# Gated linear attention and a GELU MLP on one core: two more pairs' q' and k' transposed by DMA, their decays computed a block earlier

## The chip, the cores and the metric

The kernel runs on one NeuronCore of a Trainium2 chip. The metric is the device time of one execution in microseconds (us), lower is better. Beside it stands a profile: one execution recorded by the hardware profiler, with every instruction of every engine. The engines are TensorE (PE; its weight loads are listed as PEld), VectorE (DVE), ScalarE (ACT), GpSimd (POOL) and SyncE (SP). SP and POOL only issue DMAs here, apart from a few small instructions of POOL. Each engine runs its own list of instructions strictly in the order in which they were emitted.

## The reference, cut to what matters

Inputs are q, k, v and alpha, each of shape 4 x 8 x 768 x 48 (batch, heads, steps, head size), and two weight matrices, 384 x 2048 and 2048 x 384.

```python
for t in range(S):
    state = alpha[:, :, t, :, None] * state + einsum('bhd,bhe->bhde', k[:, :, t], v[:, :, t])
    y[:, :, t] = einsum('bhd,bhde->bhe', q[:, :, t], state)
x = y.transpose(0, 2, 1, 3).reshape(B * S, H * D)
h = x @ w_in
g = 0.5 * h * (1.0 + tanh(c * (h + 0.044715 * h**3)))
return g @ w_out
```

A recurrence with a decay per step and channel runs over 768 steps; its outputs, 8 heads x 48 = 384 numbers a step, go through a two-layer MLP with GELU.

## The kernel before, in words

The 768 steps are cut into six chunks of 128. A *pair* is one chunk of two batches, so there are 12 pairs, numbered m = 0 to 11. For each pair the recurrence is turned into matrix products:

- `ln` and `exp` (ACT): la = ln(alpha), summed over the steps by a triangular product (`cum`, PE), then b = exp(cum), binv = exp(-cum), and bend, the decay over the whole chunk. `ln` and `exp` need another activation table than GELU, and a table load stands between.
- `qp`, `kp` (DVE): q' = q b and k' = k binv (line 408).
- `turn`: q' and k' are transposed, head channels to partitions. For most pairs TensorE does it, 16 transposes of 128 x 128 for a pair (line 418), and DVE or ACT copies the result out of PSUM (`ev`, line 436). For the pairs in `TURN_QK` (7 to 11 before) SP issues two DMA transposes instead (`turn_dma`, line 456), one for q' and one for k'; TensorE and DVE then do nothing for it.
- `attn` (PE, line 479): scores of k' and q' within the chunk; `mask` (DVE, line 486) makes them triangular; `y` (PE, lines 533 and 536) adds the part of the state and the part within the chunk; `kv` (PE, line 496) and `st` (DVE, lines 518 and 521) carry the state on.
- `x`: y is copied to bf16 (line 543) and transposed, either by TensorE with a DVE copy (`tx`, `xe`, lines 550 and 554) or, for the pairs in `TURN_X`, by a DMA transpose from SP (line 462).
- The MLP for the pair's 256 tokens, called a *block*: `l1` (line 562), eight groups of six products, each followed by a GELU of 128 x 512 on ACT (line 568); `l2` (line 581), 32 products of 128 x 384, then a copy `ot` (line 593) and a store from SP (line 599).

The order of instructions isn't written as loops. `tasks()` makes a list of tasks with a cost for each engine that may run it, a priority, the tasks it depends on, and the buffers that it takes. `Scheduler.order()` then plays the engines against each other with these costs and emits the tasks in the order in which they would start. The priority of attention work of pair m is about 100 m, that of the MLP is 10000 and more, so that attention work goes first as soon as it can and the MLP fills the rest. The first part of the program (to about 31 us) is not planned but written out, in `FIRST`: `P:fill.5` there means five products of zeros on TensorE. After that the planner puts in products of zeros itself where it sees TensorE idle, up to its time 60 us.

Three tables set what the change is about. `DECAYS` says after which block's GELUs the `ln` and `exp` of which pairs are run: `4: (6, 7)` means that pairs 6 and 7 follow the last GELU of block 4, and the first GELU of block 5 waits for them. `TURN_QK` and `TURN_X` choose the crossbar of the DMA or TensorE for the transposes. The planner's guess when a DMA transpose has landed is in `put`:

```python
if t.kind in ("turn", "store"):
    xbar = t.done = max(xbar, t.end + W["landed"] - t.xbar) + t.xbar
    t.done += t.late
```

with 1250 ns for the issue, 2200 for `landed`, and `late` on top. On the chip the instruction that reads the result waits for the DMA's semaphore, whatever the planner guessed.

The inputs come in by DMAs that POOL issues (line 298: a, q, k and v of a pair), one after the other, until about 91 us. Buffers bound how far they run ahead: six of `a`, five each of `q` and `k`, six of `vb`; q' and k' live in rings of four (`qp`, `kp`), the transposed q' and k' in four of `qkT`, the sums of ln(alpha) in one PSUM buffer `ca`.

Of the kernel before, what the change touches and what calls it, by code (L numbers as in the profile page):

```python
# [14 lines left out]
W = dict(**{'in': 2400},  # L15
    ln=760, exp=720, bend=170, gelu4=510, gelu2=340, table=1290,
    cum=530, cum_packed=1500, t8=450, t4=225, attn=340, kv=170, inter=170, intra=205, tx=168, l1_4=655, l1_2=340, l2=655,
    qk2=910, qk1=500, ev8=650, ev4=350, mask=640, st=1090, st0=545, end=110, attn2=590, vb=320, vb_act=480, ring=1300, ring_issue=670, out=2050, lead=600, receipt=1400, receipt_hw=1000, xc=520, xe=330, ot=540,
    ev8_act=960, ev4_act=520, xc_act=450, xe_act=450, ot_act=450,
    strip=1700, cast=1900, weight=2080, dma=2100, issue=1100, wissue=760, sp=100, store=2600, turn=1250, landed=2200, xbar_qk=1500, xbar_x=1000, late_x=2500, late_qk=1200, piece=330, late_k=1500, piece_issue=450, begin=620, cast_0=1300, share=1200, cast_1=1900, ln_packed=1040, cold=380, fill=216, zero=1100,  # L20
)
COST = {
    ("ACT", "b"): (385, 135), ("ACT", "binv"): (385, 135), ("ACT", "ev"): (600, 40), ("ACT", "gelu"): (510, 110),
# [148 lines left out]
class _Kernel:  # L172

    BLOCKS = ((0,), (1,), (2,), (3,), (4,), (5,), (6,), (7,), (8,), (9,), (10,), (11,))
    DECAYS = {-1: (0, 1), 1: (2, 3), 2: (4,), 3: (5,), 4: (6, 7), 5: (8,), 6: (9,), 7: (10,), 8: (11,)}

    SPLIT = (2,)
    EARLY = (0, 1)
# [3 lines left out]
    RINGS = (('a', 0, 0, 1), ('a', 0, 1, 2), ('q', 0, 0, 1), ('k', 0, 0, 1), ('q', 0, 1, 2), ('k', 0, 1, 2),  # L182
             ('a', 1, 0, 1), ('a', 1, 1, 2), ('q', 1, 0, 1), ('k', 1, 0, 1), ('q', 1, 1, 2), ('k', 1, 1, 2))
    FIRST = """
        A:table.0 S:load.0 S:load.1 S:load.2 S:load.3 S:load.4 A:ln0.0 S:load.5 P:fill.5 P:cum0.0 A:ln0.1 G:gate.0 G:load.12 S:load.6 P:cum0.1 A:b0.0 S:load.7
        A:binv0.0 V:qp0.0 A:bend0.0 A:b0.1 V:kp0.0 S:load.8 P:fill.2 P:t0.0 A:bend0.1 A:binv0.1 V:ev0.0 P:t0.1 S:load.9 A:ev0.1 S:load.10 V:qp0.1 P:fill.3
        P:attn0.0 V:kp0.1 P:t0.2 G:gate.1 S:load.11 G:load.13 V:mask0.1 P:fill.1 P:t0.3 G:load.14 A:ev0.3 V:end0.0 V:ev0.2 A:ln1.0 V:mask0.0 P:fill.4
        P:attn0.1 G:load.15 P:cum1.0 V:mask0.2 A:vb0.0 G:load.16 A:ln1.1 V:vb0.1 P:y0.0 V:mask0.3 A:b1.0 P:cum1.1 G:load.17 A:x0.0 V:qp1.0 A:binv1.0 P:y0.1
# [13 lines left out]

    NARROW = (0, 1)

    TURN_QK, TURN_X = (7, 8, 9, 10, 11), (6, 7, 8, 9, 10, 11)

    EV_ACT = (0, 1, 2, 3)

# [393 lines left out]
    def tasks(self):  # L602
        s = self.s = Scheduler(self.BUFS, self.fill, 60000, self.FIRST, self.LANDED)
# [6 lines left out]
        loads, n, gate, held = {}, 0, [], {}  # L610
# [26 lines left out]
        for step in self.LOADS:  # L637
            if step[0] == "v":
                rows(int(step[1:]), "v")
            elif step[:4] == "gate":  # L640
                r, m, j = step[4:].split()
                m, j = int(m), int(j)
                gate = [s.add("gate", {"POOL": 150}, n, self.wait(r, m, j), [loads[r, m, j]] if (r, m, j) in loads else [])]
# [10 lines left out]
        for m, (c, i) in enumerate(pairs):  # L654
            u, P = self.p[c, i], 100 * m
# [5 lines left out]
            for lo, hi in self.parts(m):  # L661
                n = hi - lo
                ln = s.add("ln", {"ACT": W["ln_packed" if u["packed"] else "ln"] * n // 2}, P, self.ln(u, lo, hi), [loads["a", m, lo]], LN_EXP)
                cum = s.add("cum", {"PE": W["cum_packed" if u["packed"] else "cum"] * n // 2}, P - 400, self.cum(u, lo, hi), [ln])
                x = [s.add(e, {"ACT": W[e] if e == "bend" else W["exp"] * n // 2}, P + 2 + j, self.exp(u, e, lo, hi), [cum], LN_EXP)
                     for j, e in enumerate(("b", "binv", "bend") if u["sums"] else ("b", "binv"))]
                cums.append(cum)
                exps += x
                lns[m].append(ln)
                if u["sums"]:  # L670
                    be.append(x[2])
                ends[m].append(x[-1])
                step = 1 if early else n
                for j in range(lo, hi, step):
                    qp[j:j + step] = [s.add("qp", {"DVE": W[f"qk{step}"]}, P + (5 + 4 * j if u["packed"] else 5 + 5 * j), self.scaled(u, "q", j, j + step),
                                            [x[0], loads["q", m, j]])] * step
                for j in range(lo, hi, step):
                    kp[j:j + step] = [s.add("kp", {"DVE": W[f"qk{step}"]}, P + (6 + 4 * j if u["packed"] else 6 + j), self.scaled(u, "k", j, j + step),
                                            [x[1], loads["k", m, j]])] * step
            for r, ts in (("qp", qp), ("kp", kp)):  # L680
                for j in range(2):
# [14 lines left out]
            exps[0].take("b8", *qp, *kp)  # L696
            vs, kvs, tq, cs, users, turns, masks = [], [], [], [], [], [], {}
            if m in self.TURN_QK:
                tq = [s.add("turn", {"SP": W["turn"]}, P + 10, self.turn_dma(u, n), d, xbar=W["xbar_qk"], late=W["late_qk"] * (m < 8)) for n, d in (("q", qp), ("k", kp))]
                owner, turned = tq[0], tq  # L700
            backs = []
            vin = [loads["v", m, j] for j in range(2)]
# [4 lines left out]
            for j in range(2):  # L707
                o, k = P + 10 + 3 * j, kp[j]
                if m not in self.TURN_QK:
                    turned = []  # L710
                    o -= 3 * u["packed"]
                    for which in ("q", "k") if early else ("qk",):
                        n = 4 * len(which)
# [22 lines left out]
            for j in range(2):  # L736
                b, o, k, ms, turned = 2 * i + j, P + 10 + 3 * j, kp[j], masks[j], turns[j]
# [16 lines left out]
                if c < NCH - 1:  # L754
                    if u["packed"]:
                        tb = s.add("t", {"PE": W["t4"]}, P + 29 + j, self.turn_back(u, j), turned)
                        k = s.add("ev", {"DVE": W["ev4"], "ACT": W["ev4_act"]}, P + 29 + j, self.turned_back(u, j), [tb])
# [30 lines left out]
        n = 0  # L788
        f, gs, l2s, ots, parts_of, firsts = {}, {}, {}, [], [], []
        between = {m: [x for p in self.DECAYS.get(m, ()) for x in ends[p]] for m in range(-1, len(self.BLOCKS))}  # L790

# [17 lines left out]
        def layer2(m):  # L809
            nonlocal n  # L810
            s.scope = m
            units = [(pairs[p][0], 2 * pairs[p][1] + j) for p in ((0, 1) if m == 0 else self.BLOCKS[m]) for j in range(2)]
            parts = range(self.NFT // 4)
            first = {}
            for u, part in ([(u, part) for part in parts for u in units] if m == 0 else [(u, part) for u in units for part in parts]):
                c, b = u
                t = s.add("l2", {"PE": W["l2"]}, 10000 + n, self.layer2(f, c, b, part),
                          gs[m if m else b // 2][2 * part:2 * part + 2] + [loads["w", "out", part]] + firsts, stream=n - 16)
                l2s.setdefault(c, []).append(t)
                n += 1  # L820
                first.setdefault(u, t)
                if (c, b) == (NCH - 1, B - 1):
                    t.deps += gs[m]
                    if part % 2 == 0:
                        parts_of.append(t)
                    if part % 2:
                        ot = s.add("ot", {"DVE": W["ot"], "ACT": W["ot_act"]}, -1, self.result(f, c, b, part // 2), [t])
                        ots.append((ot, s.add("store", {"SP": W["sp"]}, n, self.store(f, c, b, part // 2), [ot])))
                        parts_of[part // 2].take("ff", ot)
                        if part == 3:  # L830
                            ots[0][0].take("ot", *[x[1] for x in ots])
                elif part == parts[-1]:
                    ot = s.add("ot", {"DVE": W["ot"], "ACT": W["ot_act"]}, -1, self.result(f, c, b), [t])
                    first[u].take("ff", ot)
                    ot.take("ot", s.add("store", {"SP": W["sp"]}, n, self.store(f, c, b), [ot]))

        for m in range(len(self.BLOCKS)):
            layer1(m)
            if m:
                layer2(m if m > 1 else 0)  # L840
        for m, ps in self.DECAYS.items():
            for p in ps if m >= 0 else ():
# [57 lines left out]
```

## Time and profile before

| What | Value |
|---|---|
| median of three runs | 179.37 us (179.23, 179.37, 179.83) |
| the profiled execution's own time | 179.62 us |
| its span, first to last instruction | 177.8 us |
| granted TensorE clock, mean | 0.997 |
| layer 1, 576 products of 128 x 256 | 68.8 us busy |
| layer 2, 400 products | 69.4 us busy |
| GELU, 96 of 128 x 512 | 56.1 us busy |
| transposes of q' and k' by TensorE, 112 | 227 and 226 ns each, 5.7 us busy for each of q' and k' |
| activation table loads, 18 | 1283 ns each |
| a load of a, q, k or vb issued by POOL | 11.7 to 12.2 us to landing (median) |

How to read it: busy time is summed for an engine, and the engines work side by side, so the shares don't add up to the span. A product listed at 273 ns overlaps the one behind it; what it costs TensorE is the distance from its start to the next one's start, which the chain of work that ended last shows better. Time to landing is counted from when the DMA's issue starts.

### The profile page before, as it was taken

To read this page: it belongs to the slowest core of one execution; us is meant where nothing else is said; L and a number is where in the kernel's file an instruction comes from. 1 tells how busy PE (TensorE), PEld (TensorE's weight loads), DVE (VectorE), ACT (ScalarE), POOL (GpSimd) and SP (SyncE) were. 2 spreads that over 40 slices of the span, in tenths; PEclk is the share of its full clock that TensorE was granted. 3 is DMA by queue.
4 is the path that set the end of the run, shared out by engine and by line. 5 is a ranking of instruction groups with operands and counts; after the bars stand their busy time and mean duration, and the time that the engine had idled before them with its cause. 6 is when DMAs were issued, how large, how long until landed. Compare 5 with 4: busy or idle time off the path is not lost.

```text
span 177.8 us, 4409 instructions
## 1 busy us (share of the span) xinstructions
PE 172.0 (97%) x1829; PEld 136.1 (77%) x1831; DVE 95.0 (53%) x187; ACT 130.8 (74%) x216; POOL 58.0 (33%) x64
## 2 busy tenths in 40 slices
PE   5999999999999999999999999999999999999992
PEld 1756899666896897798698689688697697786972
DVE  6399820254967894597499797495426405000000
ACT  4558899875898668858788967987988984481831
POOL 2377536996647676667640000000000000000000
PEclk9999999999999999999999999999999999999998
DMA  4999999999999999999999993271270360401102
GB/s 124 277 253 198 196 233 232 224 240 197 231 295 195 219 269 217 191 254 210 195 248 237 197 168 85 55 177 48 46 208 4 89 162 4 129 4 48 44 3 86
DMA packets 48901, 28.86 MB, mean 162 GB/s; under 512 B 37489, under 2 KB 45297, under 8 KB 48881
## 3 DMA queue, kind: packets, MB, share of 16 engines
q0 software_dynamic: 26464, 17.70, 60.7%
q1 hardware_dynamic: 22416, 10.88, 24.7%
q8 instruction: 14, 0.23, 0.6%
q14 instruction: 7, 0.05, 0.1%
HBM read 25.17 MB, written 4.72 MB: 168 GB/s over the span
## 4 chain that ended last, share of the span: by engine, by line
PE 90%; DVE 3%; ACT 3%; issue 1%; POOL 0%; POOLq 0%
PE acc L581 35%; PE hT L562 34%; PE at L479 4%; PE qkT_ps L418 4%; PE yps L536 2%; PE cum L368 2%; PE yps L533 2%; PE kv L496 2%; PE cum L336 2%; PE idle L279 1%; DVE atm L486 1%; ACT qkT L436 1%; PE xT_ps L550 1%; ACT L568 1%; PE cum L370 1%
## 5 line engine op out<-in xcount | busy, mean ns | idle before, releaser
L581 PE MATMUL acc<-w_out,gT 128*128 128x384 bf16 (+1 forms) x400 | 69.4, 320 | 0.0
L562 PE MATMUL hT<-xT,w_in 128*128 128x256 bf16 x576 | 68.8, 273 | 0.1
L568 ACT ACTIVATE gT<-hT 128x512 bf16<-128x512 f32 x96 | 56.1, 599 | 15.1 <-PE hT L562 11.6
L562 PEld LDWEIGHTS <-w_in 128*128 128x128 bf16 x576 | 61.2, 113 | 1.5 <-issue 0.2
L581 PEld LDWEIGHTS <-gT 128*128 128x128 bf16 x400 | 36.5, 97 | 18.9
L486 DVE TENSOR_TENSOR atm<-at,ut 128x512 bf16<-128x512 f32 x48 | 30.2, 684 | 13.9 <-PE at L479 13.9
L408 DVE TENSOR_TENSOR qp<-q,b 128x768 bf16<-128x768 f32 (+1 forms) x15 | 11.9, 795 | 17.9 <-ACT b L397 17.9
L593 ACT COPY ot<-acc 128x384 f32<-128x384 f32 (+1 forms) x18 | 8.3, 460 | 13.8 <-PE acc L581 11.5
L298 POOL DMA_DIRECT2D q<-in_q_dram x11 | 12.2, 1108 | 7.3 <-DMA w_out<-in_moe_w_out_dram 1.9
L298 POOL DMA_DIRECT2D k<-in_k_dram x11 | 12.3, 1119 | 6.6 <-DMA vb<-in_v_dram 2.2
L298 POOL DMA_DIRECT2D vb<-in_v_dram x11 | 12.1, 1103 | 5.8 <-DMA a<-in_alpha_dram 2.0
L298 POOL DMA_DIRECT2D a<-in_alpha_dram x11 | 12.2, 1113 | 5.4 <-DMA w_in<-in_moe_w_in_dram 1.3
L397 ACT ACTIVATE b<-cum 128x768 bf16<-128x768 f32 (+1 forms) x15 | 10.2, 683 | 3.1 <-PE cum L340 1.6
L270 ACT ACT_TABLE_LOAD x9 | 11.5, 1283 | 0.9 <-PEq L884 0.7
L408 DVE TENSOR_TENSOR kp<-k,binv 128x768 bf16<-128x768 f32 (+1 forms) x15 | 11.9, 791 | 0.0
L568 ACT ACT_TABLE_LOAD x9 | 11.5, 1283 | 0.2
L397 ACT ACTIVATE binv<-cum 128x768 bf16<-128x768 f32 (+1 forms) x15 | 10.2, 681 | 0.0
L518 DVE TENSOR_TENSOR stmp<-kv,st 128x384 f32<-128x384 f32 x16 | 8.9, 553 | 2.0 <-PE kv L496 2.0
L543 DVE CAST x<-yps 128x384 bf16<-128x384 f32 x12 | 6.7, 558 | 5.2 <-PE yps L536 5.2
L351 ACT ACTIVATE la<-a 128x768 f16<-128x768 f32 (+1 forms) x11 | 8.5, 783 | 1.1 <-DMA a<-in_alpha_dram 1.0
L521 DVE TENSOR_TENSOR st<-stmp,ends 128x384 bf16<-128x384 f32 x16 | 8.9, 558 | 0.6
L436 ACT COPY qkT<-qkT_ps 128x512 bf16<-128x512 bf16 (+1 forms) x9 | 6.5, 728 | 3.6 <-PE qkT_ps L418 3.5
(64 smaller groups left out, 158.8 us busy)
## 6 DMA issues: line engine op xcount, KB each, us to landing
out_dram<-ot SPq DMA_DIRECT2D x23, 192.0 KB, 2.4
a<-in_alpha_dram POOLq DMA_DIRECT2D x9, 384.0 KB, 12.2
q<-in_q_dram POOLq DMA_DIRECT2D x9, 384.0 KB, 11.7
k<-in_k_dram POOLq DMA_DIRECT2D x9, 384.0 KB, 11.8
vb<-in_v_dram POOLq DMA_DIRECT2D x9, 192.0 KB, 11.9
w_in<-in_moe_w_in_dram POOLq DMA_DIRECT2D x4, 384.0 KB, 9.2
w_out<-in_moe_w_out_dram POOLq DMA_DIRECT2D x4, 384.0 KB, 11.7
a<-in_alpha_dram SPq DMA_DIRECT2D x4, 192.0 KB, 4.0
```

The costliest lines, as they stand in the source:

```text
L270: nc.scalar.add_instruction(mybir.InstLoadActFuncSet(name=nc.get_next_instruction_name(), act_func_set_id=i, engine=mybir.EngineType.Activ ...
L298: dma(u[t][:, lo:hi].rearrange("t b h d -> t (b h) d"), src.rearrange("b h s d -> s (b h) d")[c * C:(c + 1) * C])
L351: self.nc.scalar.activation(u["la"][:, lo:hi, :, 0:self.D], u["a"][:, lo:hi], AF.Ln)
L397: self.nc.scalar.activation(u[n].rearrange("t i h d -> t i (h d)")[:, lo:hi], cum, AF.Exp, scale=1.0 if n == "b" else -1.0)
L408: self.nc.vector.tensor_tensor(out, rows, b, op=ALU.mult)
L486: self.nc.vector.tensor_tensor(u["atm", i][:, o], u["at", i][o], self.ut[:, None, :].to_broadcast([self.C, self.H // 2, self.C]), op=ALU.mult)
L518: nc.vector.tensor_tensor(s, acc, old, op=ALU.add)
L521: nc.vector.tensor_tensor(new.rearrange("f p (o d) -> f (p o) d", o=2), acc.rearrange("f p (o d) -> f (p o) d", o=2), ends, op=ALU.mult)
L562: self.nc.tensor.matmul(h[:, s], w_in[:, j, nt % 4 + s], self.xT[c % self.NX][:, j, lo:hi].rearrange("p g t -> p (g t)"), start=j == 0, st ...
L568: return lambda e: self.nc.scalar.activation(self.gT[c % self.NG][:, nt:nt + 2, lo * self.C:hi * self.C], f.pop(("h", c, lo, nt)), AF.Gelu ...
L581: self.nc.tensor.matmul(f["acc", c, b][:, lo:hi], self.gT[c % self.NG][:, nt, b * self.C:(b + 1) * self.C], self.w_out[:, nt, lo:hi], star ...
L593: self.copy(e)(f["ot", c, b][:, sl], f["acc", c, b] if half is None else f["acc", c, b, half][:, sl])
```

## The change

The `ln` and `exp` of pair 5 are moved from after block 3 to after block 2, beside those of pair 4; those of pair 6 from after block 4 to after block 3; those of pair 7 stay after block 4, now alone. The q' and k' of pairs 5 and 6 are transposed by DMA. The x of pair 6, which was transposed by DMA, is transposed by TensorE. The `qp` and `kp` tasks of pairs 5 and 6 get a priority that is 90 lower in number, which is near that of the pair before. The planner's `late` is 7500 ns for q' and k' of pairs 5 and 6 and 3500 for those of pair 7, in place of 1200 for pair 7 alone. The first group of products of zeros has seven in place of five.

```diff
-    DECAYS = {-1: (0, 1), 1: (2, 3), 2: (4,), 3: (5,), 4: (6, 7), 5: (8,), 6: (9,), 7: (10,), 8: (11,)}
+    DECAYS = {-1: (0, 1), 1: (2, 3), 2: (4, 5), 3: (6,), 4: (7,), 5: (8,), 6: (9,), 7: (10,), 8: (11,)}
...
-        A:table.0 S:load.0 S:load.1 S:load.2 S:load.3 S:load.4 A:ln0.0 S:load.5 P:fill.5 P:cum0.0 A:ln0.1 G:gate.0 G:load.12 S:load.6 P:cum0.1 A:b0.0 S:load.7
+        A:table.0 S:load.0 S:load.1 S:load.2 S:load.3 S:load.4 A:ln0.0 S:load.5 P:fill.7 P:cum0.0 A:ln0.1 G:gate.0 G:load.12 S:load.6 P:cum0.1 A:b0.0 S:load.7
...
-    TURN_QK, TURN_X = (7, 8, 9, 10, 11), (6, 7, 8, 9, 10, 11)
+    TURN_QK, TURN_X = (5, 6, 7, 8, 9, 10, 11), (7, 8, 9, 10, 11)
+
+    AHEAD = {5: 90, 6: 90}
+    LATE = {5: 7500, 6: 7500, 7: 3500}
...
-                    qp[j:j + step] = [s.add("qp", {"DVE": W[f"qk{step}"]}, P + (5 + 4 * j if u["packed"] else 5 + 5 * j), self.scaled(u, "q", j, j + step),
+                    qp[j:j + step] = [s.add("qp", {"DVE": W[f"qk{step}"]}, P - self.AHEAD.get(m, 0) + (5 + 4 * j if u["packed"] else 5 + 5 * j), self.scaled(u, "q", j, j + step),
...
-                    kp[j:j + step] = [s.add("kp", {"DVE": W[f"qk{step}"]}, P + (6 + 4 * j if u["packed"] else 6 + j), self.scaled(u, "k", j, j + step),
+                    kp[j:j + step] = [s.add("kp", {"DVE": W[f"qk{step}"]}, P - self.AHEAD.get(m, 0) + (6 + 4 * j if u["packed"] else 6 + j), self.scaled(u, "k", j, j + step),
...
-                tq = [s.add("turn", {"SP": W["turn"]}, P + 10, self.turn_dma(u, n), d, xbar=W["xbar_qk"], late=W["late_qk"] * (m < 8)) for n, d in (("q", qp), ("k", kp))]
+                tq = [s.add("turn", {"SP": W["turn"]}, P + 10, self.turn_dma(u, n), d, xbar=W["xbar_qk"], late=self.LATE.get(m, 0)) for n, d in (("q", qp), ("k", kp))]
```

The entry `late_qk=1200` goes out of the table of costs.

More of the change, by code (lines that the diff above doesn't have):

```diff
@@ L19 @@
     ev8_act=960, ev4_act=520, xc_act=450, xe_act=450, ot_act=450,
-    strip=1700, cast=1900, weight=2080, dma=2100, issue=1100, wissue=760, sp=100, store=2600, turn=1250, landed=2200, xbar_qk=1500, xbar_x=1000, late_x=2500, late_qk=1200, piece=330, late_k=1500, piece_issue=450, begin=620, cast_0=1300, share=1200, cast_1=1900, ln_packed=1040, cold=380, fill=216, zero=1100,
+    strip=1700, cast=1900, weight=2080, dma=2100, issue=1100, wissue=760, sp=100, store=2600, turn=1250, landed=2200, xbar_qk=1500, xbar_x=1000, late_x=2500, piece=330, late_k=1500, piece_issue=450, begin=620, cast_0=1300, share=1200, cast_1=1900, ln_packed=1040, cold=380, fill=216, zero=1100,
 )
```

## The prediction

> **What bounds the kernel now.** I read the page first: the busy shares, the forty slices, the chain that ended last.
>
> ```profile
> span 177.8 us, 4409 instructions
> ...
> PE 172.0 (97%) x1829; PEld 136.1 (77%) x1831; DVE 95.0 (53%) x187; ACT 130.8 (74%) x216; POOL 58.0 (33%) x64
> ...
> PE   5999999999999999999999999999999999999992
> ...
> DMA  4999999999999999999999993271270360401102
> ...
> PE 90%; DVE 3%; ACT 3%; issue 1%; POOL 0%; POOLq 0%
> ```
>
> TensorE has no idle slice between the first and the last, and it is 90% of the chain; the DMA engines are as full over the first 24 slices (to 107 us). A busy TensorE may still hide stalls, so I took the busy time by stretch, and then the chain around one pair.
>
> ```profile
> 60.00:75.00 15.00, 15.00 (x172) 12.24 (x170) 10.38 (x21) 11.93 (x17) 9.65 (x9) 1.00 1.30 228
> 75.00:89.00 14.00, 14.00 (x170) 11.24 (x169) 9.62 (x20) 10.26 (x16) 9.34 (x9) 1.00 1.53 218
> ```
>
> (Columns: length, then busy of PE, weight loads, DVE, ACT, POOL; granted clock, DMA share, GB/s.) TensorE is never idle there. In the chain the sixth pair (pair 5, counted from 0) reads:
>
> ```profile
> 74.45 0.66 PE hT L562 x6
> 75.10 0.89 PE qkT_ps L418 x16
> 76.00 0.66 PE hT L562 x6
> 76.65 0.17 PE kv L496 x4
> 76.82 0.65 PE hT L562 x6
> 77.48 0.55 PE at L479 x16
> ```
>
> Sixteen transposes cost 0.89 us, 56 ns each, with layer-1 products (109 ns each) straight before and behind: product after product. So from 23 us to the last product, at 174.6 us, an instruction taken off TensorE is its issue time gained, if nothing it waits for comes later.
>
> The start is different: there the chain names products that run slowly.
>
> ```profile
> 7.17 0.88 PE idle L279 x2
> 8.04 0.85 PE qkT_ps L418 x8
> 8.90 1.04 PE idle L279 x3
> ...
> 14.79 0.38 PE idle L279
> ```
>
> Two products of zeros take 0.88 us (0.44 each) and eight transposes 0.85 (106 ns, against the 56 ns above). By the timeline four such products take 1.03 us at 10.87. The array runs at half speed until some time between 9 and 10.9 us; the windows view doesn't show that (it says 1.00 there), the durations do.
>
> **What the Trainium skill says.** (1) "TensorE: Matmul & The Clock Gate", Part 1: the array starts at half clock and is released after about 3.4 us of sustained activity, counted in windows that run freely. The trace agrees in kind: 0.44 us a product, then about 0.22. (2) "DMA: Bandwidth & Descriptors", section "Queues, rings and completion order": each DMA engine takes turns between the queues that have work for it. That bears on transposes among loads; the trace shows only SP's stores there (6.2 to 7.5 us to land against 2.1 later), which fits. No other page decides anything below.
>
> **The change part by part.**
>
> *q' and k' of pairs 5 and 6 by the crossbar.* TensorE loses 2 x 16 transposes (L418): 2 x 0.89 = 1.78 us. DVE loses four evictions (L436, 0.69 us each). SP gains four transposes, 1.2 to 1.4 us of issue each; its stores are too sparse there (57.2, 61.1, 71.9, 75.1, 85.9) for them to be pushed late by more than about that. *x of pair 6 back on TensorE* (TURN_X): 2 x 3 transposes, "0.17" each three by the chain, +0.34 us; DVE gains two copies (L554, 0.35 each), SP loses two transposes. Net: TensorE -1.78 + 0.34 = -1.44 us; DVE -2.76 + 0.70 = -2.1 us, off the chain.
>
> *Decays a block earlier* (DECAYS). The nine phases of ln and exp, each with two table loads of 1.28 us, stay nine: pair 5 joins pair 4's, pair 6 and pair 7 get one each. ScalarE can't run GELU in a phase, so TensorE lives on what doesn't need it. Now pair 4's phase is 53.51 to 61.07 (table load to table load), of which 1.41 us is idle ("issue"). The two-pair phase at 82.61 to 89.90 is 7.29 us and the single one at 68.66 to 73.46 is 4.80, so a second pair costs 2.5 us; against 1.41 idle the phase grows by about 1.1 us. TensorE's work beside it is layer 2 of block 2 (32 products of 162 ns, 5.2 us), pair 3's y and x, two cums, pair 4's transposes, and layer-1 groups as banks allow; two-pair phase 82.61 shows no TensorE idle with the same mix. Cost 0 to 0.9 us, taken 0; the phase around 83 us gives 2.5 us of ScalarE back. Buffers: `ca` has one buffer, so pair 5's cum waits for pair 4's exps (0.89 us in the phase at 83), inside the phase. Pair 5's alpha was issued at 41.85 and a load takes 12 to 13 us, so it is there at about 54.8, just in time for ln at about 55.5; q and k follow by 58.5.
>
> *AHEAD*: pair 5's qp and kp (0.95 us each on DVE) get the priority of pair 4's. They may delay an eviction or mask of pair 4 by up to 0.95 us; TensorE has layer-1 work then. Taken 0, at worst 0.5.
>
> *LATE, the new wait.* Scores (L479) of pairs 5 and 6 now wait for a DMA. In line 110 a transpose counts as done 1.25 (issue) + 2.2 us after it starts, plus `late`: 7.5 gives 10.95 us from issue. TensorE runs in order: if it lands later, layer 1 and 2 behind the scores wait too. Pair 5's k' is issued at about 63 to 64 (its b and binv at about 60, then DVE), scores due about 75; now they run at 77.4. What is known among loads:
>
> ```profile
> out_dram<-ot SPq DMA_DIRECT2D x1, 192.0 KB, 7.5
> ...
> xT<-x SPq DMA_TRANSPOSE x1, 5.9
> ...
> qkT<-qp SPq DMA_TRANSPOSE x1, 2.8
> qkT<-kp SPq DMA_TRANSPOSE x1, 2.7
> ```
>
> (The store issued at 57.2, the x transpose at 95.1 while loads still flow, and q', k' at 116 without them.) Loads add 5.4 us to a store (7.5 - 2.1) and 3.6 to an x transpose (5.9 - 2.3). From below: 2.8 + 3.6 = 6.4 us; from above, with q' before k' and one such delay each, 2.8 + 2 x 5.4 = 13.6 from the first issue, some 12 from the second. Against 10.95 I take "lands in time": stall 0, with up to 1 us in the range and the worse end as a rival. Pair 7's 3.5 gives 6.95 us, and its transposes go out near the end of the loads (the last were issued at 90 and take 10 to 12); taken 0. The four transposes also take turns from the loads; those of pairs 8 to 11 land 10 us and more before their ln, so that costs nothing.
>
> *Seven products of zeros.* Five take 1.19 to 3.50; then TensorE idles 0.76 us until the mask and la are ready at 4.26. Two more at 0.43 end their streaming at about 4.18: cost 0 to 0.1. In return TensorE is busy without a break from 1.19 instead of from 4.26. If the release then comes before 7.0 instead of at 9 to 10, the two products at 7.17 cost 0.44 instead of 0.88: the transposes, started at 7.84, are then bound by kp (done at 7.37) and start at 7.43; the first four take 0.22 instead of 0.43. DVE's first eviction moves from 8.51 to about 7.9: 0.6 us, handed on by the chain of DVE, ScalarE and TensorE up to 23 us, and with qp of the first pair the gate that lets the weights be loaded moves too. Where the free-running window falls decides it: 0 to 0.9, taken 0.6.
>
> *Sum* against the profiled execution: 177.8 - 1.44 - 0.6 = 175.75 us of span. Around the span lie 179.62 - 177.8 = 1.82 us: 177.57. The median of the runs (179.37) is 0.25 under the profiled one: 177.3; forecast **177.4 us**.
>
> **The rivals.**
>
> *Late landing (slower).* The place: TensorE at the scores of pairs 5 and 6. For it: at 103.4 us, after the loads, a 16 KB instruction fetch of 1.4 us fell on one DMA engine. Counted in 0.1 us steps, the packet records show the q' transpose moving 504 packets of 256 bytes, about 32 on each of 16 engines, then almost nothing until 105.5. So a transpose waits for its slowest engine every 32 packets or so. q' and k' of a pair are 64 + 64 per engine: four rounds. Loads add 4.1 to 5.4 us to a store on its slowest engine; if every round paid that, k' would land 19 us or more after q' was issued, some 17 after its own issue, against 10.95: 6 us late. Against it: the 24 packets per engine of the x transpose at 95 went through with 3.6 us of delay in all, and rounds may overlap. At half that, about 2.5 to 3 us per pair: 177.4 + 5 = **182.5 us**. It decides once both stalls together exceed 2 us.
>
> *Given back.* The two-pair phase costs its 0.9, a landing is 0.5 to 1 us late and the clock isn't released earlier: -1.44 + 0.9 + 0.7 = +0.2 us: **179.4**. For it: three terms that the profile can't exclude. Against: no TensorE idle in the two-pair phase that exists.
>
> *The plan isn't what the diff says.* All queues are planned anew, so a different order of loads or a fill product (0.22 us each, only before 60 us) may appear: 0.2 to 0.4 us either way, inside the ranges.
>
> **How the numbers follow.** In time and released earlier: 0.53, own range 176.6 to 178.3. Given back: 0.11, 178.3 to 180. Late landing: 0.36, 180 to 185. About 0.3% (0.54 us) is what a measurement of this kernel can tell from no change: 178.83 to 179.91. Faster takes the first case and a quarter of the second, 0.55; same 0.08; slower 0.37. For 8 in 10 the range leaves out a few hundredths below 176.6 and reaches up through most of the late case: 176.6 to 183.
>
> **What would show it.** L418 with 32 transposes fewer for q and k, L550 with 6 more. TensorE busy 100% in every stretch from 46 to 103: right; a wait of at (L479) on a DMA, or an idle gap at 74 to 78 or 86 to 92: the late rival, of the size of the gap. q' and k' transposes on SP at about 62 to 64 and 73 to 76 with times to landing under 11 us: right. The first transposes of q at about 7.4 instead of 7.84 and products of 0.22 us before 8: the start's 0.6. The forecast is wrong if k' of pair 5 takes over 12 us to land, or if GELU after the two-pair phase starts with TensorE idle.

## The result, and the profile after

The changed kernel takes 192.03 us (median of six runs, 190.19 to 199.60) against 179.56 us for the kernel before beside it: a ratio of 1.068, interval 1.062 to 1.073. The forecast was 177.4 us, and its range ended at 183.0. Some executions of a kernel, whichever it is, run some per cent longer than the rest, here those of 196.69 and 199.60 us: the ratios and intervals in this document leave such executions out, the medians don't. The profiled execution was the one of 199.60 us, so the profile shown is from a second set of runs of the same kernel (192.83 us, ratio 1.074, interval 1.070 to 1.079; its profiled execution took 193.34 us). The change has put three lines in ahead of the code, so its line numbers stand three above those before: 421 the transposes, 459 the DMA transposes of q' and k', 482 the scores, 565 and 584 layers 1 and 2.

The page after. The rows with forty characters are slices of 4.8 us here.

```profile
span 191.6 us, 4368 instructions
...
PE 174.8 (91%) x1807; PEld 135.7 (71%) x1807; DVE 92.8 (48%) x185; ACT 130.5 (68%) x216; POOL 57.9 (30%) x64
...
PE   7999999999999998299992299999999999999993
...
PEclk9999999999999999979999559999999999999999
DMA  4999999999999999999999983614327053220102
...
PE 77%; DMA 16%; ACT 3%; DVE 1%; issue 0%
```

TensorE has two holes, at slices 16 and 21 to 22. Behind each, the granted clock falls (the 7, then 5 and 5). In the chain of work that ended last TensorE's share has fallen from 90% to 77%, and a DMA holds 16%. TensorE is busy for 2.8 us longer, although it runs 22 products fewer: it has less work and does part of it at a lower clock. The windows say the same in numbers (columns as in the prediction: length, busy of PE, weight loads, DVE, ACT and POOL, then granted clock, DMA share, GB/s).

```profile
75.00:89.00 14.00, 9.27 (x100) 7.32 (x99) 6.07 (x13) 6.17 (x10) 3.44 (x3) 0.88 1.46 181
...
103.00:117.00 14.00, 8.16 (x72) 4.97 (x73) 3.14 (x6) 2.82 (x6) 0.00 (x0) 0.63 1.06 143
...
80.80:84.20 3.40, 3.37 (x27) 2.26 (x20) 3.32 (x6) 0.60 (x1) 0.39 (x1) 0.50 1.69 145
104.70:114.90 10.20, 6.06 (x43) 3.46 (x43) 2.48 (x4) 0.88 (x2) 0.00 (x0) 0.50 1.09 142
```

From 75 to 89 us, where TensorE was busy for all 14 us before, it is idle for 4.7. The last two windows lie on the stretches in which the records show half the clock. Now what the scores waited for (us in total, times, longest), and the chain of work that ended last at the two holes (start, length, what):

```profile
PE at L482 <- DMA qkT<-kp: 11.8, 2, 7.1
```

```profile
64.06 16.30 DMA qkT<-kp
80.36 0.05 issue
80.41 0.71 PE at L482 x16
81.12 0.43 PE kv L499 x4
...
81.59 3.39 PE hT L565 x18
...
94.47 14.31 DMA qkT<-kp
...
108.84 1.04 PE at L482 x16
109.87 3.95 PE acc L584 x12
```

The first hole, 4.7 us, is the wait of pair 5's scores for k', which was issued at 64.06 and took 16.30 us to land. The second, 7.09 us, is that of pair 7's (14.31 us). Pair 6 doesn't wait: its k' landed at 90.15, when the wait for pair 5 had already put everything behind it late. Which pair waits how long changes from one execution to the next: in that of 199.60 us it was 1.44, 4.26 and 9.40 us for pairs 5, 6 and 7. What follows a wait is slow: 18 layer-1 products take 3.39 us where 18 at full clock take 2.0 (six take 0.67 just behind), and 12 of layer 2 take 3.95 us instead of 1.95.

The group of the DMA transposes of pairs 5 to 7 (columns: duration of the *issue* on SP in ns, smallest, median, largest; then first and last start):

```profile
L459 SPq DMA_TRANSPOSE qkT<-qp x3: 1339/1439/3521, 62.5 to 93.0; - x3
L459 SPq DMA_TRANSPOSE qkT<-kp x3: 4105/7018/8588, 64.1 to 94.5; - x3
...
DMA to landing us min/median/max: 11.0/13.7/16.3
```

Later, without loads, the same transposes land in 2.7 to 2.8 us, and SP is held 1.3 us by each. The loads that POOL issues between 60 and 75 us have changed as well: their time to landing was 11.7/12.3/12.6 us before (smallest, median, largest) and is 11.5/18.9/21.0 after. The last load lands at 112.7 us, before at 100.7.

### The profile page after: what moved, and what is told of

Read it like the earlier page. It is cut to its first block, busy times and chain, and to the rows that moved or that the text cites. A ratio compares the mean times of both kernels' runs of the same rounds, so it can differ in the third digit from the quotient of the medians.

```text
span 197.8 us, 4366 instructions
## 1 busy us (share of the span) xinstructions
PE 174.9 (88%) x1805; PEld 136.2 (69%) x1807; DVE 93.0 (47%) x185; ACT 130.3 (66%) x216; POOL 57.9 (29%) x64
## 4 chain that ended last, share of the span: by engine, by line
PE 63%; DMA 29%; SPq 4%; ACT 2%; issue 0%; DVE 0%; DVEq 0%
PE acc L584 27%; PE hT L565 25%; DMA qkT<-kp 24%; DMA k<-in_k_dram 4%; SPq L298 4%; PE at L482 3%; PE qkT_ps L421 2%; PE yps L539 1%; PE cum L371 1%; PE yps L536 1%; PE kv L499 1%; ACT L571 1%; PE k_ps L447 1%; PE cum L373 0%; PE xT_ps L553 0%
## 5 line engine op out<-in xcount | busy, mean ns | idle before, releaser
L584 PE MATMUL acc<-w_out,gT 128*128 128x384 bf16 (+1 forms) x400 | 72.0, 327 | 0.0
L565 PEld LDWEIGHTS <-w_in 128*128 128x128 bf16 x576 | 62.1, 114 | 2.1 <-issue 0.6
L584 PEld LDWEIGHTS <-gT 128*128 128x128 bf16 x400 | 37.1, 99 | 20.5 <-issue 2.4
L596 ACT COPY ot<-acc 128x384 f32<-128x384 f32 (+1 forms) x19 | 8.8, 463 | 32.5 <-PE acc L584 32.1
L482 PE MATMUL at<-qkT 64*128 64x128 bf16 x192 | 8.6, 229 | 15.3 <-DMA qkT<-kp 15.1
L482 PEld LDWEIGHTS <-qkT 64*128 64x128 bf16 x192 | 5.8, 99 | 19.6 <-DMA qkT<-kp 16.3
L546 DVE CAST x<-yps 128x384 bf16<-128x384 f32 x13 | 7.3, 558 | 12.9 <-PE yps L539 12.7
L273 ACT ACT_TABLE_LOAD x9 | 11.5, 1283 | 0.9 <-PEq L887 0.7
L571 ACT ACT_TABLE_LOAD x9 | 11.5, 1283 | 0.2
## 6 DMA issues: line engine op xcount, KB each, us to landing
vb<-in_v_dram POOLq DMA_DIRECT2D x9, 192.0 KB, 12.3
```

What stands on the lines that cost most here:

```text
L273: nc.scalar.add_instruction(mybir.InstLoadActFuncSet(name=nc.get_next_instruction_name(), act_func_set_id=i, engine=mybir.EngineType.Activ ...
L482: nc.tensor.matmul(at[o][:, p, :], t[sl, 1, p, :], t[sl, 0, p, :], start=True, stop=True)
L565: self.nc.tensor.matmul(h[:, s], w_in[:, j, nt % 4 + s], self.xT[c % self.NX][:, j, lo:hi].rearrange("p g t -> p (g t)"), start=j == 0, st ...
L571: return lambda e: self.nc.scalar.activation(self.gT[c % self.NG][:, nt:nt + 2, lo * self.C:hi * self.C], f.pop(("h", c, lo, nt)), AF.Gelu ...
L584: self.nc.tensor.matmul(f["acc", c, b][:, lo:hi], self.gT[c % self.NG][:, nt, b * self.C:(b + 1) * self.C], self.w_out[:, nt, lo:hi], star ...
L596: self.copy(e)(f["ot", c, b][:, sl], f["acc", c, b] if half is None else f["acc", c, b, half][:, sl])
```

## The experiments

The questions were: whether the landing among loads is the cause, and all of it; why it takes so long; and whether the change's other parts cost or give what the prediction said. The first idea was that the transfers are late and the planner allows them too little time. Its rival: transfers and loads hold each other up, so that more allowance cures nothing. All ratios are to the kernel before, run beside.

**Seven products of zeros alone.** On the kernel before:

```diff
-... P:fill.5 P:cum0.0 ...
+... P:fill.7 P:cum0.0 ...
```

> The kernel before with seven products of zeros instead of five at the first place, nothing else. Theory of the prediction: the clock is released earlier and about 0.6 us is gained (0 to 0.9): 178.6 to 179.6 us. Rival: the point of release moves with the free-running window and nothing is gained that can be measured: 179.2 to 179.8.

Measured: 178.65 us against 179.47, ratio 0.9952 (0.9939 to 0.9966). The chain that ended last, near 8 us:

```profile
7.51 0.40 PE qkT_ps L418 x4
7.90 0.65 PE idle L279 x3
...
8.58 0.40 PE at L479 x8
```

The transposes of the first pair start at 7.51, and the products of zeros behind them take 0.22 us each, not 0.44. In the clock's records the release to full clock comes at 6.0 us instead of 9.6. This part gives 0.8 us; the prediction took 0.6.

**All of the change but the transposes among loads.** On the kernel after:

```diff
-    TURN_QK = (5, 6, 7, 8, 9, 10, 11)
+    TURN_QK = (8, 9, 10, 11)
```

> The changed kernel with no q' and k' by the crossbar before the ninth pair: the sixth, seventh and eighth pairs' are transposed by TensorE. Decays a block ahead, priorities, x of the seventh pair by TensorE and the seven products stay. Theory A (the rest of the change is harmless): seven products -0.8, the eighth pair's 16 transposes +0.9, the seventh's x +0.3: about 179.9 us, 179.3 to 180.5. Theory B (the two-pair phase of decays or the new order costs too): 181 us or more, with TensorE idle near 60 us.

Measured: 179.47 us, ratio 1.0005 (0.9992 to 1.0019), 12 runs. Its windows:

```profile
75.00:89.00 14.00, 14.00 (x172) 11.52 (x171) 11.81 (x23) 8.23 (x14) 9.21 (x8) 1.00 1.37 225
...
103.00:117.00 14.00, 14.00 (x148) 10.96 (x147) 8.82 (x15) 11.86 (x19) 0.00 (x0) 1.00 0.40 89
```

TensorE is full in both. The decays a block ahead, with pairs 4 and 5 in one phase, and the earlier q' and k' cost nothing by themselves. (Against the kernel before this one saves the 0.8 us of the start and has 16 transposes of pair 7 and six of pair 6's x more on TensorE, +1.2 us by the prices of the prediction; the 0.4 us left over don't show.) So without the DMA transposes of pairs 5 to 7 the loss is gone.

**Pairs 5 and 6 on TensorE, pair 7 left.**

```diff
-    TURN_QK = (5, 6, 7, 8, 9, 10, 11)
+    TURN_QK = (7, 8, 9, 10, 11)
```

> The changed kernel with q' and k' of the sixth and seventh pairs transposed by TensorE again; decays a block ahead, x of the seventh pair by TensorE, the planner's 3.5 us for the eighth pair and the seven products stay. Theory A (the transposes of these two pairs among the loads are the whole loss, and what they do to the eighth pair's): about 180 us, 179 to 182, and the eighth pair's k' lands within 8 us. Theory B (the rest of the change, above all the eighth pair's transposes a block ahead with the 3.5 us, costs too): 183 us or more, with TensorE idle before the scores of the eighth pair.

Measured: 184.64 us, ratio 1.027 (1.025 to 1.030). The chain near the second hole:

```profile
93.78 14.48 DMA qkT<-kp
...
108.30 1.04 PE at L482 x16
109.34 1.40 PE hT L565 x6
```

Pair 7 alone costs 5 us. TensorE waits 6.00 us, and then runs at half clock until 112.4 us. (The profiled execution, 187.06 us, is the longest of the four: its mean granted clock is 0.978, that of the others 0.987 to 0.990.) Before, pair 7 was transposed by DMA too, and nothing waited: by the times of its DMAs q' was issued at 97.05 us and k' at 99.70, while the last load landed at 100.67, and they took 4.79 and 3.41 us. Here, with pair 6's decays gone from its phase, they are issued at 90.94 and 93.78, into the full stream of loads, which then ends at 108.98.

**Only pair 5 among loads; and the same with the loads held back.** First, on the kernel after:

```diff
-    TURN_QK = (5, 6, 7, 8, 9, 10, 11)
+    TURN_QK = (5, 8, 9, 10, 11)
```

> The changed kernel with the crossbar for the sixth pair alone among the loads: the seventh and eighth pairs' q' and k' are transposed by TensorE; the rest of the change stays. Theory A (each pair among the loads costs by itself, since a transpose and the loads hold each other up): k' of the sixth pair lands 12 us or more after its issue, TensorE waits 0.5 to 3 us before its scores, 179 to 182 us. Theory B (the loss comes from several transposes one behind the other): k' within 9 us, no wait, 177.5 to 178.7 us.

Then, beyond that, POOL holds its list of loads at one point (a *gate*, a small instruction of POOL that waits): it issues pair 7's loads and all behind them only after pair 5's transposed q' and k' have landed (the gate reads the transposed tile and has both transposes as dependencies; of the edit only the list is shown):

```diff
-... '5', '6', '7', '8', ...
+... '5', '6', 'gateT 5 0', '7', '8', ...
```

> The kernel of e5_one, with the loads of the eighth pair and later held on POOL until the sixth pair's transposed k' has landed, so that hardly a load is in flight beside these transposes. Theory A (the loads in flight are the cause): k' lands within 5 us of its issue and TensorE doesn't wait for it; 177 to 179 us, if the loads held back 10 us don't come late elsewhere. Theory C (the landing is slow for another reason: SP's queue, its stores, the crossbar itself at this place): k' again 9 us or more.

Measured: 185.77 us, ratio 1.035 (1.030 to 1.040), and 186.81 us, ratio 1.030 (1.027 to 1.034). The first is slower than was expected of it, 179 to 182 us, since its wait is longer than the 3 us foreseen. The q' and k' transposes of pair 5, among loads:

```profile
L459 SPq DMA_TRANSPOSE qkT<-qp x1: 1432/1432/1432, 62.0 to 62.0; - x1
L459 SPq DMA_TRANSPOSE qkT<-kp x1: 9325/9325/9325, 63.6 to 63.6; - x1
...
DMA to landing us min/median/max: 14.3/15.4/16.6
```

and with the loads held:

```profile
L459 SPq DMA_TRANSPOSE qkT<-qp x1: 1333/1333/1333, 62.8 to 62.8; - x1
L459 SPq DMA_TRANSPOSE qkT<-kp x1: 1247/1247/1247, 64.3 to 64.3; - x1
...
DMA to landing us min/median/max: 3.2/3.5/3.8
```

Same pair, nearly the same moment, and only the loads held back: k' lands after 16.6 us with loads in flight, after 3.2 with hardly any. The issue on SP falls from 9.3 us to 1.2 with it. So the loads in flight are the cause of the late landing, shown by removal. In the first kernel TensorE waits 5.37 us at pair 5's scores; in the second not at all there. The total is hardly better (the two intervals overlap), and 177 to 179 us, which was expected if nothing came late elsewhere, is missed: the loads now end at 111.6 us instead of 105.9 and meet the transposes of pair 8. The chain:

```profile
105.06 7.30 DMA qkT<-kp
...
112.40 1.01 PE at L482 x16
113.41 1.40 PE hT L565 x6
```

TensorE waits 3.62 us there, and again the products behind it run slowly. The wait was moved, not removed: the loads have to flow at some time.

The packet records say why a landing takes so long. Packets that started in each us, by kind (a load's packets of q, k and a have 3.4 or 4.2 KB; those of vb, which is written as bf16, 96 bytes; the transpose's 256 bytes; the two transposes together are 2048 packets on 16 engines):

```
         pair 5 among loads                      loads held back
us    transpose  load 3-4 KB  load 96 B      us    transpose  load 3-4 KB  load 96 B
66        55         47            0         63         0          1          684
67        75         55            0         64       370          0          390
70        88         38           45         65       796          0           25
71         3          4            0         66       882          0            0
75       419          0          449
76       438          0          435
```

Transpose and loads move almost one packet for one: with pair 5 among loads 358 beside 306 from 66 to 71 us, both columns of load packets counted, and 419 beside 449 and 438 beside 435 where only vb flows. That is the turn-taking between queues which the Trainium skill states ("DMA: Bandwidth & Descriptors", section "Queues, rings and completion order"), and here the trace agrees. One for one is far fewer bytes for the transpose: its packet of 256 bytes takes turns with one of up to 4.2 KB, and two transposes need 128 packets on each engine. The loads pay too: vb alone starts 1394 packets at 81 us, when the transposes are done, but some 440 a us at 75 and 76. There are also pauses: at 71 us only three transpose packets start, and packets of both kinds that began at 70.4 to 71.0 take up to 1.97 us. An instruction fetch of 16 KB stands just before (69.77 to 71.07, on one engine), but it doesn't explain all of them: with pair 7 alone, packets begun at 101.5 to 102.6 take 1.5 to 2.7 us, and no fetch is in flight from 93 to 106 us. With no transposes among the loads no load packet of 3 KB or more takes over 0.6 us between 40 and 100 us. What makes the pauses isn't shown.

**More allowance.** On the kernel after:

```diff
-    LATE = {5: 7500, 6: 7500, 7: 3500}
+    LATE = {5: 11000, 6: 15000, 7: 17000}
```

> The changed kernel with the planner's late time at 11, 15 and 17 us for the sixth, seventh and eighth pairs in place of 7.5, 7.5 and 3.5: what k' was seen to take, so that the planner puts the scores where the data are there. Theory A (only the guess was too short; TensorE has other work to put there): 177 to 180 us, no TensorE idle over 0.5 us before scores. Theory B (transposes and loads hold each other up, so that loads and transposes come late whatever the plan says, and there isn't enough other work): 182 us or more, TensorE idle in other places.

Measured: 201.15 us, ratio 1.118 (1.111 to 1.124). What TensorE waited for (us in total, times, longest), and the time to landing of the loads issued from 85 to 100 us:

```profile
PE at L482 <- DMA qkT<-kp: 20.2, 3, 19.1
```

```profile
DMA to landing us min/median/max: 21.0/26.0/30.8
```

Pair 5's wait falls to 0.80 us, and one of 19.12 us appears at 106.9, for k' of pair 8. That was issued at 107.4 and landed after 18.6 us among loads that flow until 127.4. The loads issued from 85 to 100 us take 21 to 31 us to landing, against 12.5 to 15.9 in the profile after. So a longer allowance moved the wait to another pair and made it longer: transfers and loads hold each other up. That the later plan also releases buffers, and so starts loads, later is likely, but not shown here.

**Extra transposes that nobody reads.** The kernel before, with a second q' and k' transpose by DMA for pairs 4 and 5, to scratch tiles; TensorE's own transposes stay:

```diff
...
+            if m in (4, 5):
+                for n, d in (("q", qp), ("k", kp)):
+                    tq.append(s.add("turn", {"SP": W["turn"]}, P + 10, self.probe_dma(u, n), d, xbar=W["xbar_qk"]))
...
```

> The kernel before with two extra DMA transposes each for the fifth and sixth pairs: q' and k' go also by the crossbar to tiles that nothing reads, while TensorE does its own transposes as before. Nothing waits for them except SP's own order and the reuse of the q' and k' rings. It measures the landing among loads alone. Theory A (turns packet for packet, so that the time is in the number of packets among loads): k' lands 12 us or more after its issue, and loads in flight then take 3 us or more longer than the 12 us of before; the kernel's time stays within 1% of before. Rival (in the changed kernel the transposes were slow because TensorE and POOL stood still): k' lands within 9 us.

Measured: 212.37 us, ratio 1.168 (1.164 to 1.171). The four extra transposes (issue in ns, then landing), and TensorE's longest waits:

```profile
L464 SPq DMA_TRANSPOSE scratch<-qp x2: 1687/6242/10796, 59.0 to 77.1; - x2
L464 SPq DMA_TRANSPOSE scratch<-kp x2: 5116/8024/10933, 60.8 to 88.1; - x2
...
DMA to landing us min/median/max: 12.2/18.9/27.3
```

```profile
PE hT L569 <- DMA xT<-x: 12.8, 1, 12.8
PE at L486 <- DMA qkT<-kp: 12.0, 2, 7.1
```

The time was expected within 1% of before, and that was plainly wrong. Four transfers of 1024 packets each, whose data nobody reads, cost some 30 us by the ratio. The loads issued from 55 to 70 us landed after 30 to 33 us; alpha was late (a's loads are 16% of the chain), and the transposes of pairs 7 and 8, which had few loads beside them before, now met the delayed ones (their q' and k' took 14 to 22 us). So the cost isn't that of the wait on the transpose alone: the loads' own delay can cost more. The extra transposes also hold SP, and the buffers of q' and k' that they read; how much of the 30 us comes from that wasn't separated.

**Products of zeros in the waits.** A wait and the half clock behind it come together. To part them, TensorE was given products of zeros to run in the wait: first 28 on the kernel with pair 7 alone, as a task ahead of pair 7's scores:

```diff
+                    if m == 7:
+                        busy = s.add("fill", {"PE": 100}, o, self.fill(28), sum(turns[units[0]:], []))
+                        busy.take("ff", busy)
+                        at.deps.append(busy)
```

> The kernel of e2_tensor (184.64 us) with 28 products of zeros put on TensorE just before the eighth pair's scores, where it waited 6 us for k'; they take 6.0 us at full clock. Theory: the clock falls to half because TensorE stood idle, and the work behind the wait then ran at half speed for some 4 us; with the products the clock stays, and about 2 us come back: 182 to 183.5 us. Rival: the products only add to the wait or nothing changes: 184.5 us or more.

Measured: 184.98 us, ratio 1.030 (1.028 to 1.032). The chain:

```profile
100.79 6.07 PE idle L282 x28
106.86 1.95 PE acc L584 x12
108.81 0.55 PE at L482 x16
```

No wait is left, and the clock stays whole: the scores take 0.55 us, not 1.04. But k' landed at 106.48 in this execution, and the planner had put 12 products of layer 2 behind the zeros, so the zeros displaced 6.07 us where the wait would have been some 3.8, by estimate (106.48 less 102.7, when layer 2 would have ended). The time lies in the range that was named for the rival, 184.5 us or more, and isn't below the 184.64 us of the kernel without the zeros. The surplus of zeros may have taken what the clock gave, but that isn't shown. The second try put them directly ahead of the scores of pairs 6 and 7, fitted to their waits of 4.26 and 9.40 us in the execution of 199.60 us, in the kernel after:

```diff
+            for _ in range({6: 16, 7: 36}.get(u["m"], 0)):
+                nc.tensor.matmul(u["at", units[0]][0].rearrange("k p t -> k (p t)"), self.zero[:, 0:C], self.zero, start=True, stop=True)
```

> The changed kernel with 16 products of zeros straight before the scores of the seventh pair and 36 before those of the eighth, 3.5 and 7.8 us, inside the waits of 4.3 and 9.4 us of its profile; they write the scores' own PSUM bank, which the scores overwrite. Theory (a part of the loss is the clock, which falls to half because TensorE stands idle; in the profile it was at half for 10.2 us, about 4.5 of them work): 2 to 3 us faster than the changed kernel, 188.5 to 190 us, granted clock over 0.99. Rival (the wait is everything, the clock falls for another reason): 191 to 192.5 us, clock about 0.965.

Measured: 195.78 us, ratio 1.086 (1.084 to 1.089). The chain:

```profile
95.25 3.45 PE at L478 x16
98.71 0.55 PE at L484 x16
...
107.34 7.77 PE at L478 x36
```

That is slower than either range that was expected (188.5 to 190 and 191 to 192.5). Pair 6's 3.45 us replaced no wait in this execution (its k' had landed at 89.97), pair 7's ran 5.7 us past the landing of its k' at 109.41, and pair 5, which got no zeros, waited 5.29 us. A fixed number of products can't be fitted to a landing that moves by microseconds. Both tries are inconclusive for the time. In both the clock stays whole where products run in the place of a wait.

**The kernel after once more:**

> The changed kernel again, for a second profile beside that of e9_warm: 190 to 193 us, k' of the sixth, seventh and eighth pairs 12 us or more to landing, TensorE waiting for each of them, 10 to 15 us in all.

Measured: 192.83 us, the profile shown at the start. k' took 16.3, 13.0 and 14.3 us to land, as expected, and the waits were 11.8 us in all, but only two of the three pairs waited.

**Does it add up?** Start from the span with no transposes among loads, 177.8 us. Each pair moved to the DMA takes 0.89 us off TensorE; its waits come on top; and of work that runs at half clock after a wait, half of its length is extra.

| Kernel | moved | waits | work at half clock, half of it | sum | span measured |
|---|---|---|---|---|---|
| after, second profile | 3 pairs, -2.67 | 4.71 + 7.09 | (3.4 + 6.1) / 2 = 4.75 | 191.7 | 191.6 |
| pair 5 alone | -0.89 | 5.37 | 2.9 / 2 = 1.5 | 183.8 | 183.4 |
| pair 5, loads held | -0.89 | 3.62 (pair 8) | 3.4 / 2 = 1.7 | 182.2 | 182.7 |
| pair 7 alone | -0.89 | 6.00 | 4.1 / 2 = 2.05 | 185.0 | 185.3 |
| pair 7, zeros in its wait | -0.89 | 6.07 (zeros) | 0 | 183.0 | 183.8 |

Five executions agree within 0.8 us. The sums account for TensorE's time; they don't show by themselves what made the waits. Nor do the last two rows part the clock from the wait, although about 6 us are displaced in both and the half clock is in one only: the execution with pair 7 alone is the longest of its kernel, the other three have spans of 182.3 to 183.2 us, under the 183.8 with zeros. So the clock's share is worked out, not shown.

When the clock falls can be read from the records of all twelve traces. Within an execution its changes lie on a grid of 3.413 us. Take TensorE's idle time in every stretch of that grid that lies inside the program. At full clock, all 19 stretches with 1.83 us of idle time or more are followed by half clock, and none of the 587 with 1.80 us or less is. At half clock, the 26 with 0.48 us or less are followed by full clock, and none of the 20 with 0.72 us or more is. So it isn't the length of a wait that decides, but how much idle time falls into one stretch: a wait of 5.37 us cost one stretch at half clock (pair 5 alone), one of 5.29 us two (the last try with zeros), and one of 2.74 us, wholly inside a stretch, cost one as well (the kernel with extra transposes). It also says what the two products of zeros do at the start: before, the stretch from 2.74 to 6.15 us has 0.76 us of idle time, and the next one is still at half clock; with seven products that gap is closed.

## Why the prediction was wrong

Point by point, in its own order.

*q' and k' of pairs 5 and 6 by the crossbar, -1.44 us on TensorE*: right. Line 421 has 80 transposes for 112 before, the transposes of x 42 for 36, and the sums above close with 0.89 us a pair. *Decays a block earlier, 0*, and *AHEAD, 0*: right taken by themselves, by the kernel without transposes among loads; but the decays also set when pair 7's transposes go out (point 2). *Seven products of zeros, 0.6 us*: right, 0.8. Had every transfer landed in time, the span would, by estimate, have been 177.8 - 2.67 = 175.1 us; the prediction's sum was 175.75.

The step that failed is *LATE, the new wait*: "Against 10.95 I take 'lands in time': stall 0". Its own sign of being wrong, k' of pair 5 over 12 us, came true with 16.3 us. Three terms of the step were mis-sized.

1. The landing. Its upper bound, 13.6 us from the first issue, was made by adding what a store loses among loads, 5.4 us, once for each of the two transfers. Pair 5's q' took 14.5 us, and its k' landed 17.8 us after the first issue (16.3 after its own), so even the bound was too low; the stall was 4.7 us instead of 0. A delay seen on a transfer with few large packets is not a constant to add; a transpose in packets of 256 bytes pays per packet. The rival's own estimate with every round paid, "some 17 after its own issue", was nearly right in size; it was then halved, on the ground of the x transpose at 95 us, which has 24 packets an engine instead of 128 for q' with k'. Its reason, rounds of 32 packets an engine with a wait after each, isn't borne out, so that the size is partly luck: in the kernel before, the q' transpose at 116.4 us, without loads, moves its 1024 packets in one piece from 117.5 to 118.7 us.
2. Pair 7: "its transposes go out near the end of the loads ... taken 0". It has the longest wait, 7.09 us, and costs 5 us even alone. The place was read off the old kernel, where its transposes start at 97 us with the loads nearly done. In the new one, where pair 6's decays no longer stand in pair 7's phase, they start at 93, and the loads, which the transposes hold up, end at 112.7 instead of 100.7.
3. The loads. "The four transposes also take turns from the loads ... so that costs nothing." They slow vb's packets from 1394 a us to some 440, and the time to landing of the loads issued from 60 to 75 us goes from 12.3 to 18.9 us in the median. So the end of the loads moves over pair 7's transposes.

A fourth term was in no case of the prediction: after a wait TensorE runs at half clock, 4.75 us in all by the sums above. The page of the Trainium skill that the prediction cites for the start ("TensorE: Matmul & The Clock Gate", section "HAM oscillation — how this bites in real kernels") describes this too: the clock drops again when TensorE's wait for a DMA is longer than about 3.4 us. On the length of the stretches the trace agrees: 3.41 us and 10.24 us at half clock, which are one and three of the windows of 3413 ns that Part 1 of the page states. On the wait that it takes the measurement differs: 2.74 us were enough in one place, and 1.83 us of idle time in a window in another (near 16 us in the profile of 199.60 us).

The rival *Late landing* named the right cause, transposes that land late among loads, and, for pair 5, the right place; its rounds aren't what the records show. It was too small: 5 us at pairs 5 and 6, where 11.8 us of waits came at pairs 5 and 7, and 4.75 us of clock with them. *Given back* and *the plan isn't what the diff says* didn't occur.

The best version among all of these is the kernel before with seven products of zeros, 178.65 us.

What stays open: why the issue of k' holds SP for 4 to 9 us among loads (it goes when the loads go, and nothing here shows more); what makes the pauses in the packets of transposes and loads; how much of the cost comes from vb's small packets and how much from the large ones, since no run changed the size of a load's packets; and the exact share of the half clock.

## What to carry to other kernels

A DMA transpose is cheap only while little else is in flight: 3 to 4 us here with the loads held, 11 to 16 beside them in the kernel after. Price a transfer among others by its packets and turns, never by the delay that another kind of transfer showed, and ask what it does to those others. A longer allowance for a late transfer need not cure anything: here it moved the wait to another pair and made the kernel slower, 201.15 us. And TensorE's idle time can cost the time of a slow clock on top: here as soon as 1.83 us of it fell into one stretch of 3.413 us.

## What was not expected of the hardware

- The transposes slow the loads as well as the loads slow them: the time to landing of loads went from 12 to 30 us and more beside two pairs' transposes whose data nobody read.
- SP is held by the issue of a transpose among loads: up to 9.6 us for k' (the last try with zeros; 10.9 with the extra transposes), 1.2 to 1.3 without loads. SP's stores come behind it.
- Transposes and loads pause together: only three transpose packets and four of the loads start in the us from 71 with pair 5 alone, and single packets take up to 2.7 us with pair 7 alone.
- The clock changes on a grid of 3.413 us, by TensorE's idle time in each stretch: it fell after every stretch with 1.83 us or more and after none with 1.80 or less, so that even a wait of 2.74 us cost 3.41 us at half clock.
